# An attention and two-layer kernel: the second transfer of the gates is issued third, and the planner is told that early transfers take longer

## The chip, the core and the metric

The kernel runs on one core of one Trainium2 chip. Times are device microseconds (us) of that core. TensorE (PE) has two clocks, 1.2 and 2.4 GHz; the profile prints the granted clock as a share of 2.4 GHz.

## The reference, cut to what matters

For 4 batches and 8 heads, 768 steps of a gated linear attention with head size 40 run one after the other. Its result, 3072 tokens of 320 numbers, goes through two dense layers.

```
m_new  = max(f_t + m, i_t)                       # 4 x 8 running maxima
C      = exp(f_t + m - m_new) * C + exp(i_t - m_new) * outer(v_t, k_t)
n      = exp(f_t + m - m_new) * n + exp(i_t - m_new) * k_t
y_t    = sigmoid(o_t) * (C q_t) / max(|n q_t|, 1)

x = y as (3072, 320)
x = leaky_relu(x @ w_in, 0.01) @ w_out           # 320 -> 2048 -> 320
x = relu(x @ w_in2) ** 2 @ w_out2                # 320 -> 2048 -> 320
```

## The kernel before

The 768 steps are cut into 6 chunks of 128. Inside a chunk the recurrence becomes matrix products; between chunks only C and n are carried. `attention(c, ...)` does one chunk: for each of 8 groups (4 heads of one batch) it builds decay weights from the gates, multiplies them with the products of q and k, and multiplies with v. In chunk 0 a group is three steps on PE: `bc` (L841, spreads the gates over 128 partitions), `mS` (L865, q and k) and `mPV` (L882, with v); before them stands `gate_T` (L756, L757), which turns the prepared gates `G_sb` by 90 degrees. Between the steps ScalarE takes exponentials (L854) and VectorE multiplies (L868). `mU` (L945) makes the state that is carried on. The first layer (`moe_h`, L526, and `out1`, L558 to L564) runs beside the attention of later chunks, the second layer after it. Each weight goes through `weight(layer, j)`: one transfer (L471), then seven or more VectorE and ScalarE instructions (L478 to L500) that split it into two parts.

The gates come in two transfers on SP's queue (`gates_in`, L356): the first brings the columns of chunk 0, the second those of chunks 1 and 2. Both write the tile `T`: f in columns 0 to 383, i in columns 384 to 767. So the first writes 0 to 127 and 384 to 511, the second 128 to 383 and 512 to 767, and each of them reaches across columns of the other. `gate_part(0, ...)` prepares chunk 0's gates on VectorE (L418 to L434): L418 scans f and i, L429 subtracts from i in place, L430 scans into f, L431 copies f into `G_sb`, and L432 and L433 read i, f and that copy.

The order of the work is written by a planner in the kernel (`Sched`) when the program is built. Each piece of work has an engine, a planned duration, a key, what it reads and writes, and for some an earliest start (`after`, in planned ns). `forward` plays it through and gives each engine its fixed order; `backward` and 160 random rounds change the keys, and the order with the shortest planned end is kept. A transfer is planned so: it begins 1300 ns after its issue or when the one before it is through, takes its `lat` times a factor, and lands 700 ns later; at most 8 are in flight (`LANES`), and on the chip too an issue waits for the transfer eight before it. While PE has nothing to do in the plan, `forward` puts in filler products of zeros on PE (L369, from the start on, and L572); L554 clears three accumulators in the same way.

What the planner does not know is how the framework below it guards a tile: it adds waits of its own wherever it takes two accesses of one tile to overlap. The planner gives the two gate transfers separate keys (`f0`, `i0` and `f1`, `i1` and so on) and assumes that neither has to do with the other.

SP issues at the start, in this order: gates of chunk 0, q and k of group 0, weight 0, q and k of group 1, weight 1, q and k of group 2, k and v of batch 0, q and k of group 3, k and v of batch 1, second gates, o gates (two), and so on.

Of the kernel before, what the change touches and what calls it, by code (L numbers as in the profile page):

```python
# [11 lines left out]
I32 = mybir.dt.int32  # L12
# [8 lines left out]
DP = 48  # L21
CH = 128
# [37 lines left out]
class Sched:  # L60
# [13 lines left out]
    def op(self, eng, dur, key, fn, r=(), w=(), table=None, lat=0, alt=None, after=0, small=False):  # L74


        n = Node()
        dur *= self.scale.get(eng, 1)
        n.alt, n.after, n.first = alt, max(after, ORDER["pe0"]) if eng == "PE" and key > -2000 else after, (eng, dur, fn)
        n.eng, n.dur, n.fn, n.key, n.table, n.lat, n.small = eng, dur, fn, key, table, lat, small  # L80
        n.seq, n.outs, n.allocs, n.end = len(self.nodes), [], [], None
        deps, bufs = {}, {}
        for b, k in r:
            bufs[id(b)] = b
            if k in b.last_w:
                deps[b.last_w[k].seq] = b.last_w[k]
            b.readers.setdefault(k, []).append(n)
        for b, k in w:
            bufs[id(b)] = b
            if k in b.last_w:  # L90
                deps[b.last_w[k].seq] = b.last_w[k]
            for x in b.readers.pop(k, ()):
                if x is not n:
                    deps[x.seq] = x
            b.last_w[k] = n
        for b in bufs.values():
            if b.first is None:
                b.first = n
                n.allocs.append(b)
        n.bufs = list(bufs.values())  # L100
        n.bank = any(b.bank for b in n.bufs)
        n.deps = list(deps.values())
        for d in n.deps:
            d.outs.append(n)
        self.nodes.append(n)
        return n
# [57 lines left out]
    def forward(self):  # L164
# [25 lines left out]
        out, now, dma_free, done, last, small, flights = [], 0.0, 0.0, 0, 0.0, False, [0.0] * LANES  # L190
        while done < len(self.nodes):

            for e, cand in ready.items():
                if busy[e] is not None:
                    continue
                pick = None
                for _, _, n in cand:
                    for b in n.bufs:
                        if not b.live and (b.first is not n or queue[b.tag][-1] is not b or free[b.tag] <= 0):
                            break  # L200
                    else:
                        if pick is None:
                            pick = n
                        elif n.small:
                            pick = n
                        if e != "PE" or pick.small or not small or n.key > pick.key + STAY:
                            break
                if pick is None:
                    if e == "PE" and self.idle and (now < 12000 or now - last > 300) and (fill := next((f for f in self.idle if f[1].live and f[2].start is None), None)):
                        n = Node()  # L210
                        n.eng, n.dur, n.fn, n.allocs, n.seq, n.start, n.key = e, 430 if now < 6800 else 215, fill[0], [], -1, now, 0
                        n.bufs, n.deps = [], []
                        out.append(n)
                        busy[e] = n
                        heapq.heappush(at, (now + n.dur, 0, -1))
                    continue
                n = pick
                if n.alt:
                    other = n.alt[0] if e == n.eng else n.eng
                    if e != n.eng:  # L220
                        b = busy[other]
                        ahead = (b.start + b.dur - now if b else 0) + sum(x[2].dur for x in ready[other] if x < (n.key, n.seq) and x[2].eng == other)
                        if ahead + n.dur < n.alt[1] * ORDER["bias"]:
                            continue
                        n.eng, n.dur, n.fn = n.alt
                    ready[other].remove((n.key, n.seq, n))
                cand.remove((n.key, n.seq, n))
                for b in n.allocs:
                    if b.tag is not None:
                        queue[b.tag].pop()  # L230
                        free[b.tag] -= 1
                        b.live = True
                dur = n.dur
                if e == "PE":
                    dur += 85 if small and not n.small else 0
                    small = n.small
                if n.table and n.table != table:
                    table = n.table
                    dur += 1300
                b = busy[{"DVE": "POOL", "POOL": "DVE"}.get(e)] if e in ("DVE", "POOL") else None  # L240
                if b and not n.bank and not b.bank:
                    dur += SHARE * min(dur, max(0, b.start + b.dur - now))
                if n.lat:
                    dur += max(0, flights[-LANES] - now)
                n.start = now
                out.append(n)
                busy[e] = n
                heapq.heappush(at, (now + dur, 0, n.seq))
                end = now + dur
                if n.lat:  # L250
                    begin = max(end + 1300, dma_free)
                    dma_free = begin + n.lat * 1.1
                    end = dma_free + 700
                    flights.append(end)
                n.end = end
                heapq.heappush(at, (end, 2, n.seq))
# [8 lines left out]
            n = self.nodes[seq]  # L265
# [38 lines left out]
def mlstm_moe_kernel(  # L304
# [13 lines left out]
    op = sc.op  # L318
# [32 lines left out]
    GW = 3 * CH  # L351
# [3 lines left out]
    def gates_in(lo, hi, g, o, ps_, key, after=0):  # L355
        op("SP", 420, key, lambda: SP.dma_start(out=g[1](g[0]).rearrange("p (g s) -> p g s", g=2)[:, :, lo - o:hi - o], in_=gates[:, :, lo:hi].rearrange("g p s -> p g s")),  # L356
           w=[(g[0], f"{x}{p}") for x in "fi" for p in ps_], lat=250, after=after)

    gates_in(0, CH, ga, 0, (0,), -1000)
    gates_in(CH, GW, ga, 0, (1, 2), -1000, 2900)  # L360

    warm = fixed([128, 128], BF16, name="warm")
    zeros = lambda: warm.t[:, 0:1].to_broadcast([128, 512])
# [89 lines left out]
    def weight(layer, j, key):  # L453
# [14 lines left out]
        w, w2 = wt[layer, j], wt[layer, j ^ 1]  # L468
        sh = WR - n if layer == 0 else 0
        src = slice(0, n) if j % 2 == 0 else slice(WT - n, WT)  # L470
        op("SP", 420, key - 20, lambda: SP.dma_start(out=raw.t, in_=wts[layer, j // 2, :, src].bitcast(I32).rearrange("p (n w) -> p n w", w=2)), w=[(raw, 0)], lat=2.2 * n, after=0 if layer else (500, 1700)[j] if j < 2 else 4000)  # L471

# [263 lines left out]
    def attention(c, keys, ld):  # L738
# [34 lines left out]
        for b in range(B):  # L773
            kb = keys[2 * b] + (10 if c == 0 else 0)
            nt = sb("nat", [128, H * D + H * E], slots=2)
            op("SP", 420, kb - lead(2 * b), lambda nt=nt, b=b: SP.dma_start(out=nt.t, in_=nat[c, b]), w=[(nt, 0)], lat=1000, after=0 if c or b > 1 else (2400, 3200)[b])
            v = lambda nt=nt: nt.t[:, H * D:].rearrange("p (h e) -> p h e", h=H)
            if not native:
                raw = sb("qkr", [2 * D, 2, 4, CH])
# [27 lines left out]
            for hf in range(2):  # L807
                g = 2 * b + hf
                key = keys[g]
                if native:  # L810
                    full = c > 0 or g >= 4
                    if c == 0 or not g:
                        raw = sb(f"w{(11, 10, 9, 8, 15, 14, 13, 12)[g]}" if c == 0 else "X", [128 if full else DP, 2, 4, CH])
                        if full:
                            pad(lambda raw=raw: raw.t.rearrange("p a h t -> p (a h t)"), raw, 1024, -240 + g, [(raw, 0)], c > 0)
                    op("SP", 420, key - lead(g), lambda raw=raw, g=g: SP.dma_start(out=raw.t[0:DP], in_=qk0[c, g].rearrange("e (a h t) -> e a h t", a=2, h=4)), w=[(raw, 0)], lat=1150, after=(0, 1000, 2000, 2800)[g] if c == 0 and g < 4 else 0)
                    tk = [(raw, 0)] + ([(raw, "z64"), (raw, "z32")] if full else [])
                    lhs = lambda a, h, k, raw=raw: raw.t[:, a, h % 4]
                else:
                    tt = qk3[0]  # L820
                    for k in range(2):
                        op("SP", 450, kx + 0.1 + hf, lambda xd=xd, tt=tt, k=k, hf=hf: SP.dma_start(
                            out=tt.t[:, hf, :, k].rearrange("p a i t -> p a (i t)"),
                            in_=xd.t[hf, k:k + 10 - 4 * k].rearrange("(a s) d x -> (s d) a x", a=2)[0:3 * D]),
                            r=[(xd, (o, hf)) for o in range(2)], w=[(tt, (hf, k))], lat=950)
                    tk = [(tt, (hf, k)) for k in range(2)]
                    lhs = lambda a, h, k, tt=tt, hf=hf: tt.t[:, hf, a, k, h % 4]
# [281 lines left out]
```

## Time and profile before

| | us |
|---|---|
| median of 3 runs (lowest, highest) | 848.59 (844.73, 849.31) |
| profiled execution | 846.54 |
| its span, first to last instruction | 844.8 |
| PE busy in it | 826.6 |
| VectorE busy | 616.3 |
| ScalarE busy | 502.6 |
| granted PE clock, mean | 0.975 |

PE is busy 98% of the span; the profile counts a matmul at the low clock as busy too. So the page's row of the granted clock and the idle time have to be read beside the busy time. The rows below are from the trace of the profiled execution.

### The profile page before, as it was taken

The page shows a single profiled execution, that of the slowest core. Times are in us where ns is not written, and L with a number is a line of the kernel's source. Part 1 is how long each engine was busy: PE and PEld are TensorE (multiplying, and loading weights), DVE is VectorE, ACT ScalarE, POOL GpSimd, SP SyncE. Part 2 cuts the span into 40 slices and gives each one's busy share as a digit, 9 for nine tenths or more (in the row PEclk, how much of TensorE's full clock was granted, in tenths as well). Part 3 has the DMA queues.
Part 4 walks back from the last instruction along what each step waited for, and adds up shares of the span by engine and source line. Part 5 has one row for each costly group of instructions (what it writes and reads, how often), then busy time and mean ns, then how long its engine had stood idle before and what let it go on. Part 6 is the DMA issues. An engine that isn't in the chain of part 4 may idle for free.

```text
span 844.8 us, 15525 instructions
## 1 busy us (share of the span) xinstructions
PE 826.6 (98%) x5936; PEld 738.3 (87%) x5936; DVE 616.3 (73%) x1127; ACT 502.6 (59%) x1085; POOL 155.5 (18%) x178
## 2 busy tenths in 40 slices
PE   6999999999999999999999999999999999999998
PEld 3978988887887887888888888899999999999997
DVE  3397988998887779777556989975575765655555
ACT  4477757987976698697445667553343443433333
POOL 4144558233432304221000001100000000000000
PEclk7598999999999999999999999999999999999999
DMA  9367536667655646575021442000000000000000
GB/s 256 96 187 233 162 95 186 178 177 216 194 171 153 178 133 177 160 212 164 25 57 55 133 128 94 2 32 2 1 32 1 2 32 1 33 2 1 32 1 33
DMA packets 67626, 84.99 MB, mean 101 GB/s; under 512 B 4800, under 2 KB 56800, under 8 KB 67552
## 3 DMA queue, kind: packets, MB, share of 16 engines
q1 hardware_dynamic: 67552, 84.00, 34.2%
q8 instruction: 46, 0.75, 0.4%
q14 instruction: 28, 0.23, 0.1%
HBM read 67.76 MB, written 14.50 MB: 97 GB/s over the span
## 4 chain that ended last, share of the span: by engine, by line
PE 87%; DMA 4%; DVE 4%; ACT 3%; issue 1%; POOL 1%; SPq 0%; ACTq 0%; DVEq 0%; POOLq 0%
PE hp L526 21%; PE hp L659 6%; PE acc L659 6%; PE acc L558 5%; PE acc L560 4%; PE acc L559 4%; PE attS L865 3%; PE acc L563 2%; PE hp L664 2%; PE acc L664 2%; PE acc L564 2%; PE attm L724 2%; PE acc L722 2%; PE attS L722 2%; PE acc L724 2%; PE atty L724 2%
## 5 line engine op out<-in xcount | busy, mean ns | idle before, releaser
L526 PE MATMUL hp<-xH,w 128*128 128x512 f32 (+1 forms) x595 | 171.6, 386 | 1.0 <-DVE gL L535 1.0
L526 PEld LDWEIGHTS hp<-xH,w 128*128 128x128 f32 x595 | 107.1, 190 | 20.6 <-DVE gL L535 1.6
L526 PE MATMUL hp<-xL,w 128*128 128x512 f32 (+1 forms) x357 | 115.6, 380 | 0.0
L535 DVE TENSOR_TENSOR gL<-hp,gH 128x512 fp32r<-128x512 f32 (+1 forms) x103 | 66.5, 648 | 26.8 <-ACT hp L534 26.0
L533 ACT ACTIVATE gH<-hp 128x512 fp32r<-128x512 f32 (+1 forms) x103 | 58.2, 566 | 46.2 <-PE hp L526 40.0
L558 PE MATMUL acc<-gH,w 128*128 128x512 f32 (+1 forms) x206 | 80.5, 391 | 0.0
L526 PEld LDWEIGHTS hp<-xL,w 128*128 128x128 f32 x357 | 66.5, 189 | 13.2
L560 PE MATMUL acc<-gL,w 128*128 128x512 f32 (+1 forms) x206 | 77.7, 377 | 0.0
L559 PE MATMUL acc<-gH,w 128*128 128x512 f32 (+1 forms) x206 | 77.6, 377 | 0.0
L704 ACT CAST gH<-g 128x512 fp32r<-128x512 f32 (+1 forms) x82 | 50.3, 614 | 43.0 <-DVE g L703 42.9
L705 DVE TENSOR_TENSOR gL<-g,gH 128x512 fp32r<-128x512 f32 (+1 forms) x82 | 55.3, 675 | 20.4 <-ACT gH L704 19.8
L534 ACT ACTIVATE hp<-hp 128x512 f32<-128x512 f32 (+1 forms) x103 | 57.6, 560 | 0.0
L703 DVE SCALAR_TENSOR_TENSOR g<-g 128x512 f32<-128x512 f32 (+1 forms) x82 | 55.3, 675 | 1.2
L854 ACT ACTIVATE aw<-aw,cs 128x128 f32<-128x128 f32 x160 | 51.2, 395 | 7.5 <-DMA aw<-Adram 7.3
L858 POOL TENSOR_SCALAR_AFFINE_SELECT aw<-aw 128x512 f32<-128x512 f32 x40 | 34.4, 862 | 103.6 <-ACT aw L854 86.8
L560 PEld LDWEIGHTS acc<-gL,w 128*128 128x128 f32 x206 | 38.9, 189 | 7.6 <-DVE gL L535 0.2
L868 DVE TENSOR_TENSOR aw<-aw,attS 128x512 f32<-128x512 f32 x46 | 31.4, 682 | 19.1 <-PE attS L865 17.0
L559 PEld LDWEIGHTS acc<-gH,w 128*128 128x128 f32 x206 | 39.0, 189 | 6.4
L558 PEld LDWEIGHTS acc<-gH,w 128*128 128x128 f32 x206 | 39.0, 189 | 6.5
L680 ACT COPY nat<-hp 128x256 f32<-128x256 f32 x40 | 15.0, 376 | 47.2 <-PE hp L659 47.0
L563 PE MATMUL acc<-gH,w 128*128 128x512 f32 (+1 forms) x103 | 40.0, 389 | 0.0
L680 ACT COPY nat<-acc 128x256 f32<-128x256 f32 x40 | 14.9, 374 | 41.5 <-PE acc L659 41.0
(269 smaller groups left out, 2258.4 us busy)
## 6 DMA issues: line engine op xcount, KB each, us to landing
T<-Xdram SPq DMA_DIRECT2D x64, 240.0 KB
aw<-Adram SPq DMA_DIRECT2D x40, 256.0 KB
nat<-in_nat_dram SPq DMA_DIRECT2D x24, 328.0 KB
Xdram<-X SPq DMA_DIRECT2D x32, 240.0 KB
x<-in_wts_dram SPq DMA_DIRECT2D x8, 704.0 KB
X<-in_wts_dram SPq DMA_DIRECT2D x8, 704.0 KB
qkr<-in_qk_dram SPq DMA_DIRECT2D x16, 320.0 KB
x<-in_wts_dram SPq DMA_DIRECT2D x8, 576.0 KB
```

What stands on the lines that cost most here:

```text
L526: T.matmul(hp.t[:, 0:n], w.t[:, col:col + 128], x.t[:, kt, o], start=(s == 0), stop=(s == 7))
L533: op("ACT", act(n, True), key, lambda: A.activation(gH.t[:, 0:n], h(), AF.Prelu, alpha=0.01), r=[(hp, 0)], w=[(gH, 0)])
L534: op("ACT", act(n, True), key, lambda: A.activation(h(), h(), AF.Prelu, alpha=0.01), r=[(hp, 0)], w=[(hp, 0)])
L535: op("DVE", dve(n), key, lambda: V.tensor_tensor(out=gL.t[:, 0:n], in0=h(), in1=gH.t[:, 0:n].bitcast(F32), op=ALU.subtract), r=[(hp, 0), ( ...
L558: T.matmul(a[t].t[:, o], w.t[:, hc:hc + 128], gH.t[:, 0:n], start=first, stop=False)
L559: T.matmul(a[t].t[:, o], w.t[:, lc:lc + 128], gH.t[:, 0:n], start=False, stop=False)
L560: T.matmul(a[t].t[:, o], w.t[:, hc:hc + 128], gL.t[:, 0:n], start=False, stop=last)
L563: T.matmul(a[2].t[:, o], w.t[:, 640:768], gH.t[:, 0:n], start=first, stop=False)
L659: T.matmul(o, u(), v(), start=start and i == 0, stop=i == 2, skip_group_check=True)
L703: op("DVE", 1.4 * dve(n), k, lambda g=g, o=o: V.scalar_tensor_tensor(out=g.t[:, o], in0=g.t[:, o], scalar=0.0, in1=g.t[:, o], op0=ALU.max, ...
L705: op("DVE", 1.4 * dve(n), k, lambda g=g, gH=gH, gL=gL, o=o: V.tensor_tensor(out=gL.t[:, o], in0=g.t[:, o], in1=gH.t[:, o].bitcast(F32), op ...
L854: A.activation(aw.t[:, h], x[:, h], AF.Exp, bias=cs.t[:, 4 * g + h:4 * g + h + 1])
```

## The change

The second gates' transfer loses its earliest start (2900 planned ns) and has the same first key as the first. It is issued third instead of tenth. It goes ahead of the seven transfers that were third to ninth. The earliest starts of early transfers are put 300 to 400 ns later. The planner's factor for a transfer's length, 1.1 for all so far, becomes 1.4 for one that begins before 11000 planned ns and 1.15 for later ones. The planner works through the whole kernel again with these numbers, so the fixed order of every engine may change anywhere.

```diff
                 if n.lat:
                     begin = max(end + 1300, dma_free)
-                    dma_free = begin + n.lat * 1.1
+                    dma_free = begin + n.lat * (1.4 if begin < 11000 else 1.15)
                     end = dma_free + 700
...
     gates_in(0, CH, ga, 0, (0,), -1000)
-    gates_in(CH, GW, ga, 0, (1, 2), -1000, 2900)
+    gates_in(CH, GW, ga, 0, (1, 2), -1000)
...
# weight, L471
-    after=0 if layer else (500, 1700)[j] if j < 2 else 4000)
+    after=0 if layer else (900, 2100)[j] if j < 2 else 4000)
# k and v, L776
-    after=0 if c or b > 1 else (2400, 3200)[b])
+    after=0 if c or b > 1 else (2700, 3500)[b])
# q and k of chunk 0, L816
-    after=(0, 1000, 2000, 2800)[g] if c == 0 and g < 4 else 0)
+    after=(300, 1300, 2300, 3100)[g] if c == 0 and g < 4 else 0)
```

## Rows read from the trace of the kernel before

**Rows 1.** Busy time by stage: engine busy us (instructions), granted PE clock, DMA share, GB/s.
```profile
core 0: us, PE busy (x) PEld busy (x) DVE busy (x) ACT busy (x) POOL busy (x), PEclk, DMA share, GB/s
0.00:1.80 1.80, 0.70 (x2) 0.28 (x3) 0.60 (x5) 0.99 (x1) 1.06 (x8) 1.00 0.00 0
1.80:7.84 6.04, 6.04 (x16) 2.01 (x14) 2.63 (x8) 5.96 (x7) 5.27 (x8) 1.00 0.94 267
7.84:14.87 7.03, 0.00 (x1) 0.01 (x1) 0.59 (x3) 0.07 (x1) 0.00 (x0) 0.68 1.04 277
14.87:44.54 29.67, 29.67 (x147) 26.10 (x148) 14.89 (x31) 14.14 (x35) 6.07 (x8) 0.50 0.50 140
44.54:75.26 30.72, 27.41 (x244) 25.28 (x242) 26.97 (x47) 25.70 (x73) 16.08 (x24) 1.00 0.76 221
75.26:82.08 6.82, 6.67 (x29) 6.59 (x30) 5.93 (x10) 5.37 (x8) 2.66 (x4) 0.50 0.55 182
82.08:844.80 762.72, 756.05 (x5502) 678.05 (x5500) 564.74 (x1027) 450.34 (x966) 124.37 (x129) 1.00 0.31 91
```

**Rows 2.** Chain of waits, 0 to 30 us: start, length, what set the pace.
```profile
0.82 1.81 DMA T<-in_gates_dram
2.65 0.43 DVE T L418
...
5.06 0.27 DVE G_sb L431
5.33 8.86 DMA T<-in_gates_dram
14.22 0.29 DVE G_sb L432
...
14.87 0.42 PE attS L756
```

**Rows 3.** Timeline of SP's queue: start and length of each issue.
```profile
0.82 0.38 SPq L356 DMA_DIRECT2D T<-in_gates_dram  x1
1.25 0.41 SPq L816 DMA_DIRECT2D w<-in_qk_dram  x1
1.71 0.42 SPq L471 DMA_DIRECT2D x<-in_wts_dram  x1
...
5.33 0.36 SPq L356 DMA_DIRECT2D T<-in_gates_dram  x1
6.84 0.35 SPq L768 DMA_DIRECT2D og<-in_og_dram  x1
```

**Rows 4.** Waits of the first 60 us, engines and SP's queue: total, times, longest.
```profile
DVE G_sb L432 <- DMA T<-in_gates_dram: 8.7, 1, 8.7
PE attS L756 <- DVE G_sb L433: 7.0, 1, 7.0
...
SPq L768 <- DMA x<-in_wts_dram: 1.1, 1, 1.1
SPq L768 <- DMA w<-in_qk_dram: 0.7, 1, 0.7
SPq L356 <- DVE G_sb L431: 0.2, 1, 0.2
```

**Rows 5.** PE alone by half microseconds: busy (instructions), granted clock, DMA share, GB/s.
```profile
10.00:10.50 0.50, 0.00 (x0) 0.90 1.09 355
10.50:11.00 0.50, 0.00 (x0) 0.50 1.08 247
```

**Rows 6.** Chain of waits to 120 us: one group's q-k product at either clock.
```profile
17.86 2.00 PE attS L865 x8
86.83 0.96 PE attS L865 x8
```

**Rows 7.** Timeline of PE around 44 us: fillers at chunk 0's end.
```profile
42.29 1.49 PE L554 MATMUL acc<-warm 128*128 128x512 bf16 x3
44.00 0.63 PE L572 MATMUL acc<-warm 128*128 128x512 bf16 x1
```

More of the change, by code (lines that the diff above doesn't have):

```diff
@@ L470, in weight @@
         src = slice(0, n) if j % 2 == 0 else slice(WT - n, WT)
-        op("SP", 420, key - 20, lambda: SP.dma_start(out=raw.t, in_=wts[layer, j // 2, :, src].bitcast(I32).rearrange("p (n w) -> p n w", w=2)), w=[(raw, 0)], lat=2.2 * n, after=0 if layer else (500, 1700)[j] if j < 2 else 4000)
+        op("SP", 420, key - 20, lambda: SP.dma_start(out=raw.t, in_=wts[layer, j // 2, :, src].bitcast(I32).rearrange("p (n w) -> p n w", w=2)), w=[(raw, 0)], lat=2.2 * n, after=0 if layer else (900, 2100)[j] if j < 2 else 4000)
         l = sb("wl", [128, n], I32, 2)
@@ L775, in attention @@
             nt = sb("nat", [128, H * D + H * E], slots=2)
-            op("SP", 420, kb - lead(2 * b), lambda nt=nt, b=b: SP.dma_start(out=nt.t, in_=nat[c, b]), w=[(nt, 0)], lat=1000, after=0 if c or b > 1 else (2400, 3200)[b])
+            op("SP", 420, kb - lead(2 * b), lambda nt=nt, b=b: SP.dma_start(out=nt.t, in_=nat[c, b]), w=[(nt, 0)], lat=1000, after=0 if c or b > 1 else (2700, 3500)[b])
             v = lambda nt=nt: nt.t[:, H * D:].rearrange("p (h e) -> p h e", h=H)
@@ L815, in attention @@
                             pad(lambda raw=raw: raw.t.rearrange("p a h t -> p (a h t)"), raw, 1024, -240 + g, [(raw, 0)], c > 0)
-                    op("SP", 420, key - lead(g), lambda raw=raw, g=g: SP.dma_start(out=raw.t[0:DP], in_=qk0[c, g].rearrange("e (a h t) -> e a h t", a=2, h=4)), w=[(raw, 0)], lat=1150, after=(0, 1000, 2000, 2800)[g] if c == 0 and g < 4 else 0)
+                    op("SP", 420, key - lead(g), lambda raw=raw, g=g: SP.dma_start(out=raw.t[0:DP], in_=qk0[c, g].rearrange("e (a h t) -> e a h t", a=2, h=4)), w=[(raw, 0)], lat=1150, after=(300, 1300, 2300, 3100)[g] if c == 0 and g < 4 else 0)
                     tk = [(raw, 0)] + ([(raw, "z64"), (raw, "z32")] if full else [])
```

## The prediction, made before the change was run

> **What bounds the kernel now.** I read the stages first [rows 1]. From 82.08 us to the end PE is busy 756.05 of 762.72 us at the full clock: PE is the bound there, and a microsecond won ahead of it is worth one at the end, if the work behind still arrives in time. Ahead of it three stretches stand out. From 7.84 to 14.87 PE does nothing. From 14.87 to 44.54 it is busy all 29.67 us, but at the low clock; VectorE has only 14.89 us of work in that time, ScalarE 14.14, and the DMA engines are used half. From 75.26 to 82.08 the clock is low once more.
>
> Then the chain of waits, for the idle stretch [rows 2]: it runs from the first gate transfer (landed at 2.65 by the start of L418) through VectorE's gate instructions to L431, then 8.86 us through the *second* gate transfer, then L432 to gate_T on PE at 14.87. The waits say the same: L432 stood 8.7 us for that transfer, gate_T 7.0 us for VectorE [rows 4]. L432 reads only columns of chunk 0, which the second transfer does not write; but those columns lie between the two pieces that it does write. So the framework takes the two to overlap, and the first PE step of chunk 0 waits for data that chunk 1 needs. SP's timeline shows why that data is late: issued at 5.33, tenth, behind nine larger transfers [rows 3]. The kernel's own plan has no such wait.
>
> The clock follows from the idle time. The last filler ends at 7.84; the granted clock falls at about 10.45 (0.90 as the mean of the half microsecond from 10.00, 0.50 after it) [rows 5]. It does not come back in 29.67 us in which PE never rests [rows 1], and rises at 44.54, as a run of 128x512 bf16 fillers ends that began at 42.29 [rows 7]. A group's q-k product costs 2.00 us at the low clock and 0.96 at the full one [rows 6].
>
> **The change, part by part.**
>
> *The second gate transfer, third.* It cannot simply go out at 1.71, where the third issue is now. Its reach (columns 128 to 767) overlaps the first transfer's (0 to 511) in the same sense in which L432's columns overlap it, so I expect SP to wait until the first one has landed, at 2.65, before it issues. SP's only wait at this line now is 0.2 us for a gate instruction on VectorE [rows 4], so the guard reaches SP's queue too. The Trainium skill, "DMA: Bandwidth & Descriptors", section "Two DMAs through the same engine are not ordered", speaks for this wait and against the change: a kernel that needs an order between two transfers has to hold back the second's issue until the first's completion semaphore. By it the issue stands at 2.65; without it, at 1.71; no run here shows two such transfers side by side.
>
> When does it land? The first gate transfer took 1.81 us from issue to landing [rows 2]; 2.65 + 1.81 = 4.46, and I take 4.6 because it is twice as large and has q and k of group 0 ahead of it. From both sides: 1.71 + 1.81 = 3.5 without SP's wait; and as late as the third issue of now, weight 0, which took from 1.71 to 6.84 (the o gates' issue waits for just that landing [rows 3, 4]), that is 2.65 + 5.13 = 7.8.
>
> The wait does not vanish, it moves to the head of the chain: the scan L418 reads i, so now it starts at 4.6 instead of 2.65. Behind it on VectorE stand the other gate instructions and then the first weight's, which now start after 14.5 anyway. L418 to the end of L431's step is 5.33 - 2.65 = 2.68 us, L432 to gate_T 14.87 - 14.22 = 0.65 [rows 2], together 3.3. So gate_T comes at 7.9; PE's fillers last till 7.84 [rows 1]; I take 8.0. Ends: 7.84 (fillers) and 7.8 + 3.3 = 11.1. Won at gate_T: 14.87 - 8.0 = **6.9 us** (3.8 to 7.0).
>
> *The transfers that are overtaken.* Seven lose one place: weights 0 and 1, q and k of groups 1 to 3, k and v of batches 0 and 1, and the o gates after them shift as well. Weight 0 goes from 1.71 to about 2.65 + 0.41 = 3.06: all come up to 1.35 us later, the gates' own bytes included (2 x 32 x 256 numbers of 4 bytes, 0.24 us at 277 GB/s [rows 1]). What hides it: the first that PE needs is q and k of group 1, which landed at about 7.9 (the second o issue waits 0.7 us for it, right after the first [rows 3, 4]), so at 9.2 now; PE reaches it after gate_T and three steps, each about 1.0 us at the full clock by the 0.96 of [rows 6], at 12.0. If the transfer came 2.8 us later still, PE would wait for it.
>
> *The longer planned transfers.* No instruction is added. The plan has chunk 0's steps wait longer for data, so it may put more fillers between them and order the weights' work a little later. The same holds up to the end with the factor 1.15: from 82.08 on PE idles 6.7 us in all [rows 1], so a better order can win 6.7 at most there; a worse one could lose as much. I take 0.
>
> *The clock.* With gate_T at 8.0 PE has no long pause, and the clock is still high when chunk 0 starts. If it stays high, the 29.67 us stretch is set by something else. Below: VectorE's 14.89 us. Above: 29.67, the clock stays low. I take the next stretch as the nearest row, 44.54 to 75.26, with the same kinds of work at the full clock: VectorE is busy 26.97 of 30.72 us there, 88% [rows 1], and 14.89 / 0.88 = 17.0 us. Won: **12.7 us** (0 to 14.8), ahead in all 19.6 at the end of this stretch.
>
> *What is late next.* The data. Up to 75.26 the DMA engines have moved 6.04 x 267 + 7.03 x 277 + 29.67 x 140 + 30.72 x 221 GB/s = 14.5 MB [rows 1]. At 277 GB/s, the rate with a full queue, that takes 52.3 us. Buffers don't come free fast enough to keep the queue always full: the share is 1.04 before 14.87, 0.76 from 44.54 to 75.26 [rows 1]; I take 0.9 between them. 52.3 / 0.9 = 58.1, plus 1.8 until the first bytes, plus 1.3 for the shift above, is 61.2. So the point that lies at 75.26 now cannot come much before 61.2: **14.1 us** are left of the 19.6. With a share of 1.0 it is 55.4 (19.9 won, no less than PE's own), with 0.76 it is 72.0 (3.3 won).
>
> The sum, against the profiled execution's own 846.54: 846.54 - 14.1 = 832.4. The median of the runs is 2.05 above that execution, inside their spread of 4.6, so I put the measured time at **833** and the forecast's own range at 827 to 840.
>
> **The rivals.**
>
> *The clock falls anyway.* For it: 29.67 us of nothing but small fp32 products never raised it [rows 1], so these products may not hold it either once something makes PE pause; and at 75.26 it fell in a stretch with PE 89% busy. Against it: from 44.54 to 75.26 much of the same work stood beside first-layer products at the full clock, and the new plan may add fillers. Then only gate_T's 6.9 us are won: 846.54 - 6.9 = 839.6, 841 with half of the median's offset. The Trainium skill, "TensorE: Matmul & The Clock Gate", section "Why this matters for your kernels", says that keeping TensorE busy without a break is what takes it to the full clock. By that rule this rival is out and the 14.1 us are safe; the trace does not agree, since PE was busy without a break for 29.67 us at 1.2 GHz.
>
> *Slower.* The run of fillers that raised the clock at 44.54 was placed by the old plan; the new one may scatter it. If the clock is low when chunk 0 ends and nothing raises it, the next stretch runs low as well, and each microsecond of its 27.41 us of PE work costs one more [rows 1]. It decides at 6.9 us of that work, where the loss equals what gate_T won. For half of the stretch, about 15 us: 846.54 - 6.9 + 15 = 854.6, so 855. Against it: first-layer products stand in that stretch, and the low clock that began at 75.26 was over after 6.82 us [rows 1].
>
> *The change does not do what it says.* Queued transfers could share the engines, so that a transfer issued third lands hardly earlier than the tenth; or gate_T waits for something else by then. Then 847 to 848. Against it: weight 0, a far larger transfer, landed at 6.84 from the third place [rows 3, 4].
>
> *More than forecast.* DMA and VectorE keep pace, and the second low-clock stretch (6.82 us at half speed, worth 3.4) goes away: 846.54 - 19.6 - 3.4 = 823.5.
>
> **How the numbers follow.** Forecast 0.57, clock falls anyway 0.24, no effect (or all given back) 0.07, slower 0.07, more 0.05. About 0.5% (4.2 us) is what a measurement of this kernel can tell from no change. Faster by more than that: 0.57 + 0.24 + 0.05 = 0.86; the same 0.07; slower 0.07. The range for 8 in 10 holds the forecast and the rival of the clock with its spread: 823 to 845; outside are no effect, slower and part of the last case.
>
> **What would show it.** L418 starts at about 4.6 and waits for the second gate transfer; SP has a wait of about 0.9 us ahead of the third issue; L432 follows L431 at once; gate_T stands at about 8.0; the granted clock is high through most of chunk 0, whose stretch to the first layer takes some 17 to 20 us instead of 29.67; the DMA share is near 0.9 up to 60 us. The prediction is wrong if gate_T comes after 11, if chunk 0 again runs at 0.50 (then 841), or if what is won by then is lost again behind it to late weights or a low clock.

## The result, and the profile after

| us | before | changed |
|---|---|---|
| executions | 844.73, 848.11, 848.59, 849.31 | 821.18, 821.96, 834.06, 835.07 |
| mean granted clock | 0.975 (profiled one) | 0.999, 1.000, 0.984, 0.981 |
| median | 848.35 | 828.01 |

The ratio is 0.9692 [0.9643, 0.9741]; here and below, ratios leave out executions that lie more than 1.5% above the fastest of their kernel, here the two at 834 to 835, in which the clock fell. The prediction was 833 with 823 to 845: the direction is right, but with the clock kept the kernel is 1 to 2 us below the low end. The same program, run again six times beside other kernels (called e14 below), gave 821.19, 822.15, 822.17, 827.5, 829.0 and 836.35, against a median before of 847.84; ratio 0.9737 [0.9700, 0.9774]. Its profiled execution (822.17, span 820.4, clock 0.999) is the one to read, because the clock was kept in it.

SP's queue in the changed kernel (e14); against [rows 3] the third issue now waits:

```profile
2.57 0.32 SPq L356 DMA_DIRECT2D T<-in_gates_dram  x1
2.94 0.43 SPq L471 DMA_DIRECT2D x<-in_wts_dram  x1
```

The chain of waits of the same execution (start, length, what set the pace), against [rows 2]:

```profile
0.81 1.74 DMA T<-in_gates_dram
...
2.57 2.12 DMA T<-in_gates_dram
...
4.79 0.42 DVE T L418
...
7.01 0.38 DVE T L418
7.39 0.18 DVE G_sb L432
...
7.60 0.85 DVE G_sb L431
...
8.47 0.29 DVE G_sb L433
...
8.81 0.31 PE attS L756
```

Both gate transfers now stand at the head of the chain, one behind the other, 1.74 and 2.12 us; the 8.86 us in the middle of it are gone, and gate_T starts at 8.81 instead of 14.87. A second L418 stands in the chain at 7.01: that is part 1's scan, which the new plan puts between chunk 0's instructions.

The stages of the same execution, columns as in [rows 1]:

```profile
8.81:24.77 15.96, 15.85 (x147) 13.91 (x147) 12.63 (x31) 11.91 (x31) 5.80 (x7) 1.00 1.03 291
24.77:56.22 31.45, 30.32 (x271) 28.56 (x271) 29.99 (x58) 27.58 (x79) 13.40 (x20) 1.00 0.90 265
56.22:62.95 6.73, 6.73 (x53) 6.39 (x52) 6.62 (x12) 5.44 (x7) 2.96 (x4) 1.00 0.80 254
62.95:820.40 757.45, 749.60 (x5455) 672.43 (x5453) 554.54 (x1013) 448.63 (x963) 122.00 (x134) 1.00 0.31 91
```

The stages are cut at the times of e1 below. The clock column is 1.00 in each of them: neither the 29.67 us at 0.50 nor the 6.82 at 0.50 of [rows 1] is left. Chunk 0 takes some 16 us from gate_T on.

The first changed run (834.06) has a profile too, and it shows where the time goes. PE's timeline around gate_T in it:

```profile
4.18 2.12 PE L369 MATMUL hp<-warm 128*128 128x512 bf16 x9
8.79 0.30 PE L756 MATMUL attS<-ident,G_sb 96*128 96x96 f32 x1 [2.49 <-DVE G_sb L433]
```

The same execution, PE alone by microseconds (busy (instructions), granted clock, DMA share, GB/s):

```profile
10.00:11.00 1.00, 1.00 (x10) 0.84 1.12 216
11.00:12.00 1.00, 1.00 (x7) 0.50 0.96 244
...
37.00:38.00 1.00, 1.00 (x7) 0.50 0.76 247
38.00:39.00 1.00, 0.77 (x7) 1.00 0.10 37
```

The two groups of the timeline in e14:

```profile
4.48 3.14 PE L369 MATMUL hp<-warm 128*128 128x512 bf16 x9
8.81 0.31 PE L756 MATMUL attS<-ident,G_sb 96*128 96x96 f32 x1 [1.19 <-DVE G_sb L433]
```

gate_T comes at the same time in both, but the nine fillers ahead of it took 2.12 us in the first and 3.14 in e14. The profile prints a clock of 1.00 for these first microseconds in both, so their lengths have to tell: such a filler takes 0.63 us by itself where the clock is 0.50 [rows 7], and in e14 a few of the early products of this shape still take 0.63. By this the full clock came earlier in the slower execution. PE then paused 2.49 us instead of 1.19; the clock fell at about 10.7 and was low up to 38. The number of fillers is fixed; how long they cover is not. That the longer pause is what made the clock fall is not shown by two profiles; e3, e4 and e15 bear on it.

### The profile page after: what moved, and what is told of

Same layout as the page of the kernel before. It is cut to its first block, busy times and chain, and to the rows that moved or that the text cites. A ratio compares the mean times of both kernels' runs of the same rounds, so it can differ in the third digit from the quotient of the medians.

```text
span 832.3 us, 15525 instructions
## 1 busy us (share of the span) xinstructions
PE 820.0 (99%) x5938; PEld 734.5 (88%) x5938; DVE 607.3 (73%) x1127; ACT 500.8 (60%) x1084; POOL 152.3 (18%) x179
## 4 chain that ended last, share of the span: by engine, by line
PE 83%; DMA 8%; ACT 5%; DVE 3%; issue 1%; SPq 0%; DVEq 0%; ACTq 0%
PE hp L526 19%; PE hp L659 6%; PE acc L659 6%; PE acc L558 4%; PE acc L559 4%; PE acc L560 4%; PE attS L865 3%; PE hp L664 2%; PE acc L664 2%; DMA aw<-Adram 2%; PE acc L563 2%; PE acc L564 2%; PE atty L882 2%; PE attm L724 2%; PE acc L722 2%; PE attS L722 2%
## 5 line engine op out<-in xcount | busy, mean ns | idle before, releaser
L533 ACT ACTIVATE gH<-hp 128x512 fp32r<-128x512 f32 (+1 forms) x103 | 58.1, 565 | 47.2 <-PE hp L526 45.4
L858 POOL TENSOR_SCALAR_AFFINE_SELECT aw<-aw 128x512 f32<-128x512 f32 x40 | 30.6, 766 | 81.2 <-ACT aw L854 63.4
```

The lines of the kernel that those rows point to most:

```text
L533: op("ACT", act(n, True), key, lambda: A.activation(gH.t[:, 0:n], h(), AF.Prelu, alpha=0.01), r=[(hp, 0)], w=[(gH, 0)])
```

## The experiments

The theory: the false overlap in tile `T` held gate_T back; the pause let the clock fall; chunk 0 then ran at half speed. The main rivals: the gain comes from the planner's new order, or from the transfer's place alone without the clock. In e3 and the kernels after it (e5 and e14 apart) the lines behind the edit have numbers one higher (e10: two): L883 is the L882 of before. Each kernel stands against the kernel before, run beside it on the same chip, whose median was 847.03 to 848.36.

**e1: the move alone.** The order of before, with only the second gates' transfer put third on SP.

```diff
-        for n in sc.order(PASSES):
+        plan = sc.order(PASSES)
+        late = next(n for n in plan if n.seq == second.seq)
+        plan.remove(late)
+        plan.insert(plan.index([n for n in plan if n.eng == "SP"][2]), late)
+        for n in plan:
```

> The kernel before with every engine's order as it was; only the second gates' transfer is moved, from tenth to third on SP. Theory 1 (the landing of the gates decides, through gate_T's start and the clock): SP waits at the third issue until 2.65, L418 starts at about 4.5, gate_T at 8.0 to 9.0 instead of 14.87; where the clock stays high in chunk 0 the time is 821 to 828, where it falls 834 to 842. Theory 2 (the new order of the work brings most of it, the wait little): gate_T moves as above, but the time stays at 840 to 844.

827.2 (825.18 to 827.77), ratio 0.9762 [0.9737, 0.9788], as theory 1 had it. The one transfer wins 19.8 us (847.03 to 827.2). As the order is that of before, each stage has its counterpart in [rows 1]. The stages of e1:

```profile
1.80:7.48 5.68, 5.68 (x16) 1.90 (x14) 2.48 (x9) 5.19 (x6) 5.25 (x8) 1.00 0.84 233
7.48:8.11 0.63, 0.00 (x1) 0.00 (x1) 0.56 (x3) 0.46 (x1) 0.00 (x0) 1.00 0.83 183
8.11:24.77 16.66, 16.06 (x145) 14.01 (x146) 13.19 (x30) 13.12 (x35) 5.54 (x8) 1.00 1.04 298
24.77:56.22 31.45, 27.60 (x243) 25.45 (x244) 28.18 (x50) 26.98 (x75) 17.04 (x24) 1.00 0.86 259
56.22:62.95 6.73, 6.73 (x38) 6.39 (x38) 4.81 (x9) 5.28 (x7) 2.00 (x3) 0.75 0.70 202
62.95:824.50 761.55, 754.44 (x5495) 676.81 (x5494) 561.75 (x1026) 449.94 (x965) 122.62 (x129) 1.00 0.31 91
```

And the last three stages of before, cut at the same instructions (PE's group L865 at 75.41 is the one at 56.22 in e1, its group L882 at 83.68 the one at 62.95; by then the clock is up again in both):

```profile
44.43:75.41 30.98, 27.53 (x245) 25.43 (x243) 27.23 (x48) 25.96 (x73) 16.34 (x24) 1.00 0.76 221
75.41:83.68 8.27, 8.27 (x38) 7.84 (x38) 5.80 (x10) 5.89 (x9) 3.15 (x5) 0.60 0.59 176
83.68:844.80 761.12, 754.45 (x5496) 676.76 (x5494) 564.73 (x1026) 449.67 (x963) 123.73 (x128) 1.00 0.31 91
```

gate_T 14.87 to 8.11 is 6.76 won; chunk 0's stretch 29.56 (14.87 to 44.43) to 16.66 is 12.90; the next stretch loses 0.47 (30.98 to 31.45); the stretch with the second low clock gives 1.54 (8.27 to 6.73); the rest loses 0.43 (761.12 to 761.55). Together 20.30, the difference of the spans, 844.8 - 824.5.

**e2: the new order without the move.** The changed kernel, with the transfer put back to the tenth place in the same way.

> The changed kernel with every engine's order as it is; only the second gates' transfer is put back to tenth on SP. Theory 1: L432 waits for it again until about 14, gate_T comes at about 14.5, the granted clock is 0.50 through chunk 0, and the time is 843 to 850, all of the gain gone. Theory 2: the new order keeps its gain, 828 to 838.

838.54 (834.79 to 841.88), ratio 0.9898 [0.9864, 0.9931]. gate_T stands at 15.07 again. PE's timeline from there on, in the execution of 834.79:

```profile
15.07 0.42 PE L756 MATMUL attS<-ident,G_sb 96*128 96x96 f32 x1 [7.59 <-DVE G_sb L433]
...
15.98 2.08 PE L841 MATMUL acc<-G_sb,ident 96*128 96x128 f32 x8
17.85 1.91 PE L841 MATMUL hp<-G_sb,ident 96*128 96x128 f32 x8
19.55 1.22 PE L841 MATMUL acc<-G_sb,ident 96*128 96x128 f32 x8
```

The clock in it, PE alone by stretches of two microseconds:

```profile
18.00:20.00 2.00, 2.00 (x12) 0.53 0.96 279
20.00:22.00 2.00, 2.00 (x18) 1.00 1.03 256
26.00:28.00 2.00, 2.00 (x12) 0.68 0.61 234
28.00:30.00 2.00, 2.00 (x11) 0.50 0.28 59
```

Three L841 groups one behind the other, and the clock is up by 20; at about 26.7 it falls again while PE is busy all the time. So the new order does something for the clock of its own, but without the move it is worth 8.5 us (847.03 to 838.54), less than half of what the move is worth alone. Neither theory had this: the median lies between their ranges, and the six executions part into 834.79 to 836.09 (mean clock 0.984 to 0.986) and 841.0 to 841.88 (0.978 to 0.979). Only one of the first kind has a profile.

**e3 and e4: the pause filled.** Fillers on PE directly ahead of gate_T: eight in the changed kernel (e3), 34 in the kernel before, whose gates stay late (e4).

```diff
         for n in sc.order(PASSES):
...
+            if n.seq == turns[0].seq:     # the first gate_T
+                for _ in range(8):        # e4: 34
+                    product()
             n.fn()
```

> The changed kernel with 8 more filler products of 128x512 bf16 on PE right before gate_T, nothing else. Theory 1 (the clock falls in some executions because PE pauses between the last filler, 6.30 in the profiled one, and gate_T, 8.79): the pause is under 1 us, the clock is 0.99 to 1.00 in every execution, and all times lie at 820 to 823. Rival (chunk 0's small fp32 products cannot hold the clock whatever stands before them): again executions at 833 to 836 among the others.

> The kernel before with 34 more filler products right before gate_T, which cover the 7 us in which PE waits for the gates; the gates are as late as before. It measures the clock by itself. Theory 1: gate_T at 14.2 to 15.6 as before, the granted clock high through chunk 0, whose stretch shrinks from 29.67 to about 17 to 20 us; 832 to 838. Rival (chunk 0 runs at the low clock whatever stands before it): 847 to 849.

e3: 822.65 (820.23 to 825.35), ratio 0.9713 [0.9683, 0.9742]; no execution near 834, though two lie above the 823 expected. e4: 835.51, ratio 0.9859 [0.9815, 0.9904], in two groups: 830.33 to 838.19 (clock 0.996 to 1.000), and 842.35 and 843.42 (0.981, 0.983). The stages of e4 up to gate_T, and then chunk 0's, in the execution of 830.33:

```profile
7.84:14.76 6.92, 6.86 (x32) 3.12 (x32) 1.00 (x3) 0.06 (x1) 0.00 (x0) 1.00 1.05 287
14.76:31.37 16.61, 16.01 (x146) 13.87 (x146) 13.50 (x30) 12.75 (x34) 5.61 (x8) 1.00 0.82 232
```

This parts the two terms of the prediction. gate_T is as late as before (14.76), nothing is moved, and chunk 0 takes 16.61 us instead of 29.56 (14.87 to 44.43): the clock's term alone, with the pause ahead of chunk 0 filled. In two of six executions the mean clock is as low as 0.98 all the same. They have no profile, so where it fell there, and whether the fillers had left a pause, is not known; that a filled pause always keeps the clock is not shown.

**e5 and e6: the planner's factors.** e5 is the kernel before with the factor line of the change alone; e6 is e3 with the old factor.

```diff
# e5, in the kernel before
-                    dma_free = begin + n.lat * 1.1
+                    dma_free = begin + n.lat * (1.4 if begin < 11000 else 1.15)
```

> The kernel before with only the planner's factor changed (1.4 and 1.15 for 1.1); the second gates stay tenth, the earliest starts stay. Theory 1 (what the new order is worth, 8 us with late gates, comes from the longer planned transfers): 836 to 842. Rival (it comes from the earliest starts and the gates' place in the plan, or is chance of the planner's random rounds): 844 to 852.

> The changed kernel planned with the old factor 1.1, with 8 more fillers before gate_T so that the clock stays high; to be held against the changed kernel with the same fillers (822.65). Theory 1 (the longer planned transfers are worth 4 to 5 us): 826 to 829. Rival (the factor does nothing by itself): 821 to 824.

e5: 840.95 (840.33 to 842.79), ratio 0.9925 [0.9901, 0.9948], with gate_T late and chunk 0 at the low clock (a mean of 0.51 from 15 to 44 us); the second low-clock stretch is gone. e6: 830.48 (827.99 to 834.5), ratio 0.9805 [0.9777, 0.9832], 7.8 above e3. In e6's order an L841 group and not gate_T comes first, ahead of the fillers, so a pause of 1.93 us is left before it (6.25 to 8.18); the clock was kept through that one. Taken alone, the two kernels say that the factor is worth 7 to 8 us; e11 to e13 say otherwise. The execution of 834.5 of e6 also shows the clock fall under a busy PE, here PE's timeline:

```profile
19.53 1.16 PE L866 MATMUL acc<-w 48*128 48x128 f32 x8
20.61 1.76 PE L883 MATMUL atty<-nat,aw 128*128 128x42 f32 x8
```

And the clock in it, PE alone by microseconds:

```profile
20.00:21.00 1.00, 1.00 (x10) 0.92 1.19 231
21.00:22.00 1.00, 1.00 (x7) 0.50 0.91 243
```

**e7 and e8: no overlap in the tile.** Chunk 0's f and i lie in columns 0 to 255 of `T`, those of chunks 1 and 2 in 256 to 767; the order is untouched. e7 is the kernel before so laid out (transfer still tenth), e8 the changed one.

```diff
# gates_in, the argument out alone
-    out=g[1](g[0]).rearrange("p (g s) -> p g s", g=2)[:, :, lo - o:hi - o]
+    out=(g[1](g[0]) if o else g[1](g[0])[:, 2 * lo:2 * hi]).rearrange("p (g s) -> p g s", g=2)
# gate_part, cut
-    f = lambda: ft(fb)[:, o]
-    i = lambda: ft(fb)[:, GW:][:, o]
+    fc, ic = (0, GW) if off else (0, CH) if p == 0 else (CH, GW)
+    f = lambda: ft(fb)[:, fc:][:, o]
+    i = lambda: ft(fb)[:, ic:][:, o]
```

> The kernel before, its order of work and of transfers untouched (second gates tenth); only the columns of the tile T are laid out so that neither gate transfer reaches across the other's columns (f and i of chunk 0 in columns 0 to 255, those of chunks 1 and 2 in 256 to 767). Theory 1 (the wait is one for columns that are not shared, and nothing else held chunk 0): L432 no longer waits, gate_T follows the fillers at 7.8 to 8.2, 822 to 828, clock 0.99 or more. Rival (data of chunk 0 is late as well, so the gates only hid that): gate_T early, but PE idles after it, 832 to 845.

> The changed kernel with the same layout of T, nothing else. Theory 1: SP issues the second gates at 1.7 without a wait, L418 starts at 2.65, gate_T follows the fillers with a pause under 1 us, and every execution lies at 818 to 822 with the clock at 0.99 or more. Rival (the wait for the second gates costs the changed kernel nothing, since its plan counts on late data): 821 to 823 and again some at 834.

e7: 827.19 (826.48 to 827.61), ratio 0.9760 [0.9737, 0.9782], the same as e1 without moving a transfer. gate_T on PE in it:

```profile
6.28 0.24 PE L757 MATMUL attS<-ident,G_sb 96*128 96x96 f32 x1
```

e8: 822.27 (816.53 to 826.83), ratio 0.9693 [0.9654, 0.9732]. SP's second gate issue, the first scan and gate_T in it:

```profile
1.71 0.42 SPq L356 DMA_DIRECT2D T<-in_gates_dram  x1
...
2.64 0.41 DVE L419 TENSOR_TENSOR_SCAN T<-T 32x128 f32<-32x128 f32 x1 [1.08 <-DMA T<-in_gates_dram]
...
6.83 0.29 PE L757 MATMUL attS<-ident,G_sb 96*128 96x96 f32 x1
```

SP does not wait (1.71 instead of 2.57) and the scan waits for the first transfer alone (2.64 instead of 4.79). So the wait at both places was the guard on the tile, not the hardware. Of e8's six executions three lie at 816 to 821 and three at 824 to 827, which is neither theory: none is near 834, but not all are at 822 or below. gate_T comes earlier in e7 than the 7.8 expected, since the nine fillers ahead of it took 2.12 us there. That 6.28 in e7 buys no more than 8.11 in e1 was not expected: the PE group that waits for X comes 1.6 us earlier (54.63 against 56.22), and the low clock behind it lasts longer (a mean of 0.60 from 54 to 61 and 0.93 from 61 to 70, against 0.66 from 56 to 61 and 1.00 from there in e1).

**e10: layout and fillers together.** e8 with six fillers ahead of gate_T.

> The changed kernel with the layout of T that keeps the two gate transfers apart, and 6 more fillers right before gate_T. Both waits and the pause before gate_T are gone. Theory 1 (that pause is what lets the clock fall in some executions): all executions at 816 to 821, clock 0.996 or more. Rival (the clock falls at other places too, so the spread stays): 816 to 827 as with the layout alone.

822.82 (819.65 to 826.71), ratio 0.9709 [0.9677, 0.9741]. The spread from 819 to 827 stays: a pause ahead of gate_T is not the reason for it.

**e11 to e13: factor or luck.** e11 is e3 with 1.4 for early transfers and 1.1 for late ones; e12 and e13 are e3 and e6 with another seed for the planner's random rounds (5 for 4).

> The changed kernel with 8 more fillers, planned with 1.4 for early transfers and the old 1.1 for later ones. To be held against 822.65 (1.4 and 1.15) and 830.48 (1.1 throughout), both with these fillers. If the early transfers' length carries the plan's gain: 820 to 825; if the later ones' does: 828 to 832.

> The changed kernel with 8 more fillers, with another seed for the planner's random rounds, so another order of equal planned quality. It tells the factor from luck, with the next kernel. Theory 1 (a plan with true lengths is better): 820 to 825, near 822.65. Rival (luck of the random rounds): anywhere from 819 to 832, no nearer to 822.65 than to 830.48.

> The changed kernel with 8 more fillers and the old factor 1.1, with the same other seed. Theory 1 (a plan with too short transfers is worse): 827 to 834, near 830.48. Rival (luck of the random rounds): 819 to 826 as likely as that.

| us (lowest, highest) | new factors | old factor |
|---|---|---|
| seed 4 | e3 822.65 (820.23, 825.35) | e6 830.48 (827.99, 834.5) |
| seed 5 | e12 826.99 (822.29, 833.34) | e13 824.95 (823.35, 826.84) |

e11 gave 825.09 (822.49 to 828.93), ratio 0.9736 [0.9706, 0.9766]; e12 has 0.9760 [0.9720, 0.9799], e13 0.9733 [0.9708, 0.9757]. e11 lies at the edge of the one range expected for it, 3 us from the other, and decides nothing. With the other seed the difference has no longer the same sign, and the two intervals overlap. Any change of the planner's numbers draws another order, and these orders lie up to 8 us apart; an effect of the factors themselves can't be told from that.

**e14 to e16: three versions side by side.** The changed kernel, e3 and e8 once more, on one chip.

> The changed kernel as it is, once more, beside the two that follow on the same chip. If the clock falls in chunk 0 in some executions because of the pause before gate_T, its times are again of two kinds, about 821 and about 834, and those at 834 show a mean clock of 0.98.

> The changed kernel with 8 more fillers, once more, on the same chip: all executions at 820 to 826, none at 834, if the pause is the cause.

> The changed kernel with the layout of T that keeps the gate transfers apart, once more, on the same chip: 816 to 827, none at 834; it tells whether it is better than the fillers (by 0 to 3 us).

| | median (lowest, highest) | ratio |
|---|---|---|
| e14, changed | 824.84 (821.19, 836.35) | 0.9737 [0.9700, 0.9774] |
| e15, with eight fillers | 821.51 (819.86, 827.86) | 0.9716 [0.9682, 0.9750] |
| e16, laid out without overlap | 819.67 (818.53, 826.15) | 0.9685 [0.9656, 0.9713] |

The version to keep is e16: its median is the lowest of the three, but the intervals of the ratios overlap. With the fillers (e3 and e15, ten executions) none lies above 827.86, while three of the changed kernel's ten lie at 834 or above. This speaks for the pause as what lets the clock fall there, but none of ten against three of ten is thin. e14 was not of two kinds only: 827.5 and 829.0 (mean clock 0.991 and 0.990) lie between, and e15 has two executions at 827.8 to 827.9, above its 826. What still parts 819 from 827 is the clock (0.991 to 0.992 in the slower ones of e10, e15 and e16, 0.999 to 1.000 in the fastest). e3's profiled execution shows one place where it falls, PE alone:

```profile
54.00:56.00 2.00, 2.00 (x12) 0.50 0.99 274
```

Whether it is the same place in the others stays open: only one execution of each has a profile.

Set against the move alone, the whole change is worth less than its best executions say. The ten executions of the changed kernel have a mean of 827.1 us, and the five of e1, all between 825.18 and 827.77, one of 826.8: what the new order wins where the clock is kept is lost again where it falls. The two did not run side by side, so the difference itself is not measured.

## Why the prediction was right, and where it went wrong

*The transfer, third.* Right in each part. SP held the issue until the first had landed (2.57 in e14, 2.65 predicted), it landed after 2.12 us (4.69; 4.6 predicted), and L418 waited for it. The Trainium skill, "DMA: Bandwidth & Descriptors", section "Two DMAs through the same engine are not ordered", asks for just such a held issue where two transfers depend on each other. The trace shows the wait, and e8 shows that here nothing depended: with the columns apart the issue stands at 1.71.

*gate_T.* 8.0 predicted; 8.11 in e1. In e1 the chain from L418 to gate_T takes 3.32 us, 3.3 predicted. In the changed kernel gate_T comes at 8.8: the chain takes 4.02 us, as the new plan puts part 1's scan (0.38) in front of L432, and L431 takes 0.85 instead of 0.41 in e1 (the 0.27 of [rows 2] ends where the second transfer is issued). The prediction had taken the chain as it was.

*The overtaken transfers.* Predicted as hidden. e1 bears it out: chunk 0's stretch has 16.06 us of PE work in 16.66.

*The clock.* 17.0 us for chunk 0 predicted, 16.66 measured in e1 and 16.61 in e4. The two terms add to 19.6 predicted and 19.66 measured (6.76 + 12.90). That 17.0 came so close is in part luck: it was worked out from VectorE's share, but VectorE is busy 13.19 of 16.66 us, while PE is busy 16.06. PE's own work at the full clock sets this stretch.

*The data.* **This is the step that failed** ("What is late next: the data"). It gave back 5.5 of the 19.6, so that the point at 75.26 could not come before 61.2. In e1 that point came at 56.22, and the stretch ahead of it gave back 0.47 (30.98 to 31.45). The bytes were right: 5.68 x 233 + 0.63 x 183 + 16.66 x 298 + 31.45 x 259 GB/s = 14.55 MB, 14.5 predicted. The share was right too: 0.91 over these stages, 0.9 taken. The term that was mis-sized is the rate: 14.55 MB in 54.42 us is 267 GB/s, or 293 per share of 1 (all 16 DMA engines busy), where the prediction multiplied its share by 277, taken from a stretch whose share was 1.04 (266 per share of 1). Its own rows had a higher one as well: 221 GB/s at a share of 0.76 is 291 [rows 1]. With 293, the rate as measured in e1, 14.5 MB at a share of 0.9 take 55.0 us and not 58.1. The 1.3 us for the overtaken transfers had no place beside that share: SP's wait shows as a share of 0.84 in e1's first stage (0.94 before), which is part of the 0.91. With both put right the step gives 1.8 + 55.0 = 56.8, and 56.22 was measured.

The step also took the rate of the queue for what holds the point. The chain of waits ahead of the point in e1:

```profile
48.92 1.17 PE attS L865 x8
...
50.11 5.98 DMA X<-in_qk_dram
...
56.22 1.13 PE attS L865 x8
```

And in the kernel before:

```profile
68.52 1.17 PE attS L865 x8
...
69.71 5.56 DMA X<-in_qk_dram
...
75.41 2.04 PE attS L865 x8
```

One transfer waits for a buffer that PE's products free, then takes 5.6 to 6.0 us. PE's products came 19.60 us earlier in e1 (68.52 to 48.92), so the buffer was free and the transfer issued 19.60 us earlier: a hand-over moves along with the work. This is read from the two chains; no run tried it. The transfer took 0.42 us longer in e1, and the DMA engines were busy during it in both (share 0.97 before, 0.95 in e1), so part of its length may be other transfers' bytes; how much is not shown.

*The second low-clock stretch.* The forecast left it as it was; only the rival "more than forecast" took it away, at 3.4. In e1 it gives 1.54, in e14 it is gone.

*The longer planned transfers.* Taken at nothing, with bounds of 6.7 either way. From e1 to e14 the times of the two profiled executions fall by another 4.0 (826.18 to 822.17), and the stages say where: from 24.77 to 56.22 PE does 30.32 us of work in place of 27.60, both at the full clock, and the stretch behind it, up to 62.95, has a mean of 1.00 instead of 0.75. The bounds hold this, but taking the term at nothing is a second, smaller part of the miss. That it is the factors' merit is not shown (e11 to e13).

So with the clock kept, 14.1 us were predicted and 24.4 came (846.54 to 822.17). Of the 10.3 between them, some 5.0 are the data's (5.5 charged, 0.47 lost), 1.5 the second stretch's in e1, less 0.4 lost behind it, and 4.0 come with the new order.

*The rivals.* "The clock falls anyway" (0.24, 841) does happen, in three of ten executions, at 834 to 836. The profiled one has 834.06 where the rival had 839.6: the stretch from 10.7 to 38 is about all its time at the low clock (a mean of 0.984 over 832.3 us makes 0.016 x 832.3 / 0.5 = 26.6 us), so the second low-clock stretch is gone here too. The prediction took the fall for a property of the program; it is one of the execution. Its ground for this rival, "nothing but small fp32 products" for 29.67 us, was read a little too widely: lone 128x512 bf16 products stood among them, and the last 2.1 us were the fillers of [rows 7], behind which the clock rose. "No effect" and "slower" left no trace.

By the Trainium skill, "TensorE: Matmul & The Clock Gate", section "Why this matters for your kernels", keeping TensorE busy without a break is what takes it to the full clock, and avoiding long pauses is what prevents a drop. The kernel before agrees on the pause: the clock fell within one of 7.03 us [rows 5]. e2 and e6 do not agree: the clock fell at 26.7 and 20.8 us with PE busy in every microsecond around it.

## What to carry to other kernels

A wait for a transfer whose data the waiting instruction does not read is a sign of two accesses that only enclose each other in one tile: lay the columns apart (e7), and nothing has to be moved. A pause ahead of small products can cost far more than its own length through the clock: read the granted clock behind it, and price the pause and the clock as separate terms. Before charging a gain against the data, look whether the late transfer is held by the queue or by a buffer: here the buffer came free earlier with the work, and the transfer with it.

## What the runs showed of the hardware

- The clock fell under a PE that was busy without a break, after groups of 48-row and 42-wide fp32 products (e6, 20.8 us; PE busy since 8.18). In e2 it rose just before 20, in the third of three groups of 96-row, 128-wide fp32 products that stood one behind the other; in the kernel before, where such groups take turns with the smaller ones, it was still at 0.50 when the fillers of [rows 7] began at 42.29.
- The same program's fillers at the start do not always take equally long: nine of them took 2.12 us or 3.14 us, and PE's pause before gate_T was 2.49 or 1.19, in an execution of 834.06 and one of 822.17.
- The DMA engines' rate at a share of about 1.04 was 277 GB/s in one stretch [rows 1] and 298 in another (e1); what of the mix of transfers makes the difference was not tried.
